# Where attention steps stand between the matmuls of a feed-forward layer: only after whole products, in groups, from the third run on

## The chip, the core and the metric

The kernel runs on one core of a Trainium2 chip. The core has five engines with a queue of instructions each: TensorE (PE in the profile, with PEld for the loading of its weights) does matmuls and transposes and writes PSUM; ScalarE (ACT) and VectorE (DVE) read PSUM and write on-chip memory or PSUM; GpSimd (POOL) here does pooling sums and normalisation; SyncE (SP) issues the DMAs. An engine works through its queue in order, and waits on semaphores for the others. The metric is the device time of the program in microseconds (us), less is better.

## The reference

Eight batches of attention with eight heads, whose keys and values are averaged over 8 neighbours (576 to 72), feed a two-layer network with a leaky ReLU over 4608 tokens:

```python
B, H, S, D = 8, 8, 576, 64
k_p = k.reshape(B, H, S // 8, 8, D).mean(axis=3)
v_p = v.reshape(B, H, S // 8, 8, D).mean(axis=3)
scores = np.matmul(q, k_p.transpose(0, 1, 3, 2)) / np.sqrt(D)
attn = softmax(scores)                  # max subtracted, 1e-9 added to the sum
x = heads_side_by_side(np.matmul(attn, v_p))          # 4608 x 512
h = x @ w_in                                          # 512 -> 2048
out = np.maximum(0.01 * h, h) @ w_out                 # 2048 -> 512
```

## The kernel before

**The feed-forward layer.** The tokens are cut into nine chunks of 512, the hidden width into 16 blocks `f` of 128. A block of a chunk is two products: `m1` (lines 621 to 641) makes the hidden block, twelve matmuls (four slices `kk` by three: each operand is split into a high and a low part and low times low is left out), then Prelu (L635) and a rounding copy `gh` (L638) on ACT and the rest `gl` on DVE (L639); `m2` (lines 643 to 660) adds the block's share to four accumulators, twelve matmuls as well, and comes two blocks later than the `m1` whose result it uses. Every product yields control twice: in its middle, after six matmuls (L633, L659), and at its end.

**Runs.** `runs` (L614) lists ten runs `n`: chunk 0 with blocks 0 to 7, chunk 1, chunk 0 with blocks 8 to 15, and then chunks 2 to 8, one run each. In the text "run 4, f13, m2" is the second product that is issued with block 13 of run 4.

**Attention steps.** While run `n` is at work, the attention that the next chunk needs is done in small steps, which `line_up` (L554) puts into a fixed order. The number behind the batch's name is the tile of up to 128 query rows, the last digit the half of the heads:

- `q` (L359): four transposes of a tile of q into PSUM, a copy `qT` on ACT (L365).
- `sa` (L367): four score matmuls into `pss`; DVE takes the maximum (L383), ACT takes exp, four times a pair of instructions (L385).
- `sb`: sums and reciprocals on DVE (L396, L397), normalisation `at` on POOL (L402, L406). It has no work on TensorE.
- `pu` (L417): three transposes of `at` into `pp`; from there ACT copies `pT_hi` (L429) and `rh` (L430), DVE makes `pT_lo` (L433) and `pT_rem` (L437).
- `au` (L443): for two pairs of heads each, four matmuls into `pa` that read `pT_hi`, `pT_lo`, `pT_hi` and `pT_rem` in this order (L453 to L456); ACT copies `xh` (L463), DVE makes `xl` (L464). It follows the last `pu` of its piece and half.
- `ku`, `vu` (L319, L333): keys and values of a new batch; `vu` is two pairs of matmuls into `pv` (L351), each followed by a DVE product (L354).
- `lk`, `lv`: the DMAs and POOL sums of a batch's keys and values; `fetch` and `tails` stand at the ends of run 2.

**What sets the order.** TensorE's order is the order of the source (`manual_schedule`, L749); the instructions of the other engines are put in order by the framework's scheduler. For a batch after the first every attention step takes its PSUM from one pool of two buffers (`ps_a`, L83, through `bank`, L208), in turn; `au`, `ku` and `vu` take both. `pT_hi`, `pT_lo` and `pT_rem` are single buffers. The loop at L766 counts beats, one for each yield, four for each block; at each beat it issues steps until their number reaches `len(us) * beat // (beats - 4)`. Runs 2 to 8 have 31 to 43 steps, run 2 in 32 beats, the others in 64. So before the change a beat gets one step or none, and a few beats of run 2 get two.

Of the kernel before, what the change touches and what calls it, by code (L numbers as in the profile page):

```python
# [24 lines left out]
def tile_pooled_attention_ffn(  # L25
# [595 lines left out]
    def m1(k):  # L621

        n, c, f = parts[k]
        xh, xl = x_parts(c)
        w = ws[0, f]
        nm = f"{c}_{f}"
        ph = ps_h.tile([P, CH], F32, tag="h", name=f"ph{nm}")
        for kk in range(NK):
            ks = slice(kk * P, (kk + 1) * P)
            nc.tensor.matmul(ph, w[:, 0, ks], xh[kk], start=kk == 0, stop=False)  # L630
            nc.tensor.matmul(ph, w[:, 0, ks], xl[kk], start=False, stop=False)  # L631
            nc.tensor.matmul(ph, w[:, 1, ks], xh[kk], start=False, stop=kk == NK - 1)  # L632
            if kk == 1:  # L633
                yield
        nc.scalar.activation(ph, ph, AF.Prelu, alpha=0.01)  # L635
        gh = three.tile([P, CH], F32R, tag="gh", name=f"gh{nm}")
        gl = three.tile([P, CH], F32R, tag="gl", name=f"gl{nm}")
        casts.append(nc.scalar.copy(gh, ph))  # L638
        nc.vector.tensor_tensor(gl, ph, gh.bitcast(F32), op=ALU.subtract)  # L639
        gs[k] = gh, gl  # L640
        yield

    def m2(k):

        n, c, f = parts[k]
        gh, gl = gs.pop(k)
        hi, lo = ws[1, f][:, 0, :], ws[1, f][:, 1, :]
        first, last = f == runs[n][1][0], f == runs[n][1][-1]
        for t in range(NT):
            if first:  # L650
                accs[t] = ps_acc.tile([P, DM], F32, tag=f"acc{t}", name=f"acc{n}_{t}")
            r = slice(t * P, (t + 1) * P)
            a = accs[t]
            nc.tensor.matmul(a, gh[:, r], hi, start=first, stop=False)  # L654
            nc.tensor.matmul(a, gh[:, r], lo, start=False, stop=False)  # L655
            nc.tensor.matmul(a, gl[:, r], hi, start=False, stop=last)  # L656
            if last:
                store(n, c, t, a)
            if t % 2:  # L659
                yield  # L660
# [40 lines left out]
    def convert_to(n):  # L701
        nonlocal stepped
        while stepped < min(int(n), len(steps)):
            steps[stepped]()
            stepped += 1
# [43 lines left out]
    with tc.manual_schedule(engines={nc.tensor.engine}):  # L749
        at, total = 0, len(parts)  # L750
        for n, (c, fs) in enumerate(runs):
            us = list(units[n])
            if n >= 2:
                mid = len(us) // 2
                for b in early[n]:
                    us[mid:mid] = [att[b]["lk"], att[b]["lv"]]
            beats, done, beat = 4 * len(fs), 0, 0
            for f in fs:
                if n == 0:
                    convert_to(14 + 2.8 * f)  # L760
                elif n == 1:
                    convert_to(36 + 3 * f)
                    if f == 11:
                        for b in early[1]:
                            att[b]["lk"]()
                            att[b]["lv"]()  # L766
                slots = [m1(at)] + ([m2(at - 2)] if at >= 2 else [])
                for slot in slots:
                    for _ in slot:
                        beat += 1  # L770
                        while done < min(len(us), len(us) * beat // (beats - 4)):
                            us[done]()
                            done += 1
                at += 1
            while done < len(us):
                us[done]()
                done += 1
        for at in (total - 2, total - 1):
            for _ in m2(at):
                pass  # L780
# [31 lines left out]
```

## Time and profile before

| | |
|---|---|
| runs shown | 1023.65, 1024.62, 1025.46 us; median 1024.62 |
| the profiled execution | 1024.45 us, of which 1022.7 us lie between the first and the last instruction (the span) |
| granted TensorE clock, mean | 0.971 |
| first weights and first attention, until run 2 | about 237 us |
| runs 2 to 9 | from there to the end |

The page of the profile gives busy time and share of the span for every engine, then slices, the chain of work that ended last, and groups of instructions. The timeline gives single instructions: start and duration in us, engine, line of the source, operation, output and inputs; "x3" stands for three instructions merged into one row, and a bracket says how long the engine had been idle and what released it. Matmuls overlap in it, since their ends are modelled: the pace of TensorE is read from start to start.

### The profile page before, as it was taken

What the parts mean: (1) busy time and instruction counts of PE and PEld (TensorE: products, weight loads), DVE (VectorE), ACT (ScalarE), POOL (GpSimd) and SP (SyncE); (2) the same over time, 40 slices, a digit from 0 to 9 for tenths busy, and PEclk for the clock granted to TensorE, in tenths of its full rate; (3) what the DMA queues carried; (4) which work ended last, traced back from release to release, by engine and by line L of the source; (5) the groups of instructions that cost most, each with busy time, mean ns of one, the idle gap of its engine ahead of it and who ended that gap; (6) DMA issues with size and microseconds to landing.
All of it is one profiled execution on the core that took longest, in us unless ns stands there. A gap on an engine that the chain in (4) does not pass through costs nothing.

```text
span 1022.7 us, 12812 instructions
## 1 busy us (share of the span) xinstructions
PE 963.4 (94%) x4568; PEld 785.4 (77%) x4568; DVE 363.6 (36%) x846; ACT 428.1 (42%) x1386; POOL 232.7 (23%) x336
## 2 busy tenths in 40 slices
PE   4566989989999999999999999999999999999998
PEld 4355778768887778878888788888887788888886
DVE  5787738413323332332232322232232322231111
ACT  4757755414534343534343434333443433342121
POOL 3576315520106620133012301022101001000000
PEclk8677999989999999999999999999999999999999
DMA  9556301322015410212012202020200020001001
GB/s 266 160 155 191 112 32 51 91 75 63 6 25 137 114 40 11 62 47 58 6 57 57 58 1 68 6 57 6 62 11 11 1 62 1 1 1 42 1 1 41
DMA packets 65007, 57.45 MB, mean 56 GB/s; under 512 B 39856, under 2 KB 48048, under 8 KB 64944
## 3 DMA queue, kind: packets, MB, share of 16 engines
q1 hardware_dynamic: 64944, 56.64, 19.2%
q8 instruction: 36, 0.59, 0.2%
q14 instruction: 27, 0.22, 0.1%
HBM read 46.14 MB, written 10.49 MB: 55 GB/s over the span
## 4 chain that ended last, share of the span: by engine, by line
PE 76%; DMA 2%; DVE 2%; ACT 1%; POOL 1%; issue 1%; SPq 0%; ACTq 0%; POOLq 0%; DVEq 0%
PE ph L630 12%; PE acc L654 11%; PE ph L632 11%; PE ph L631 11%; PE acc L656 11%; PE acc L655 11%; PE pss L375 3%; PE pp L427 2%; PE pq L363 1%; PE pa L453 1%; PE pa L456 1%; PE pa L454 1%; PE pa L455 1%; DVE w L196 0%; DMA kraw<-in_k_dram 0%
## 5 line engine op out<-in xcount | busy, mean ns | idle before, releaser
L630 PE MATMUL ph<-xh,w 128*128 128x512 f32 x576 | 236.9, 411 | 5.2 <-DVE gl L639 5.2
L654 PE MATMUL acc<-w,gh 128*128 128x512 f32 x576 | 234.6, 407 | 0.0
L631 PE MATMUL ph<-xl,w 128*128 128x512 f32 x576 | 227.3, 395 | 0.0
L632 PE MATMUL ph<-xh,w 128*128 128x512 f32 x576 | 227.2, 395 | 0.0
L656 PE MATMUL acc<-w,gl 128*128 128x512 f32 x576 | 225.7, 392 | 0.0
L655 PE MATMUL acc<-w,gh 128*128 128x512 f32 x576 | 225.6, 392 | 0.0
L635 ACT ACTIVATE ph<-ph 128x512 f32<-128x512 f32 x144 | 84.3, 585 | 287.4 <-PE ph L632 287.4
L639 DVE TENSOR_TENSOR gl<-ph,gh 128x512 fp32r<-128x512 f32 x144 | 99.4, 690 | 270.8 <-ACT gh L638 269.9
L402 POOL TENSOR_TENSOR at<-e,red 128x256 f32<-128x256 f32 (+1 forms) x76 | 47.4, 624 | 502.1 <-DVE red L397 370.0
L385 ACT ACTIVATE e<-pss,red 128x72 f32<-128x72 f32 (+1 forms) x320 | 98.2, 321 | 112.0 <-DVE red L383 110.9
L630 PEld LDWEIGHTS ph<-xh,w 128*128 128x128 f32 x576 | 109.6, 190 | 28.5 <-DVE gl L639 6.6
L632 PEld LDWEIGHTS ph<-xh,w 128*128 128x128 f32 x576 | 109.6, 190 | 24.3
L656 PEld LDWEIGHTS acc<-w,gl 128*128 128x128 f32 x576 | 108.4, 188 | 24.0
L654 PEld LDWEIGHTS acc<-w,gh 128*128 128x128 f32 x576 | 108.5, 188 | 21.7 <-issue 1.4
L631 PEld LDWEIGHTS ph<-xl,w 128*128 128x128 f32 x576 | 109.9, 191 | 19.5
L655 PEld LDWEIGHTS acc<-w,gh 128*128 128x128 f32 x576 | 108.7, 189 | 19.3
L638 ACT CAST gh<-ph 128x512 fp32r<-128x512 f32 x144 | 85.3, 592 | 3.0
L383 DVE TENSOR_REDUCE red<-pss 128x4 f32<-128x288 f32 (+1 forms) x80 | 36.2, 453 | 103.7 <-PE pss L375 102.7
L385 ACT ACTIVATION_READ_ACCUMULATOR e<-pss,red 128x1 f32 (+1 forms) x320 | 65.9, 206 | 0.0
L375 PEld LDWEIGHTS pss<-kT,qT 128*128 128x128 f32 (+1 forms) x320 | 49.5, 193 | 14.4 <-issue 3.5
L375 PE MATMUL pss<-kT,qT 128*128 128x144 f32 (+1 forms) x320 | 57.0, 307 | 3.0 <-ACT qT L365 1.8
L433 DVE TENSOR_TENSOR pT_lo<-pp,pT_hi 128x256 fp32r<-128x256 f32 (+1 forms) x80 | 31.6, 395 | 72.0 <-ACT rh L430 71.4
(85 smaller groups left out, 898.3 us busy)
## 6 DMA issues: line engine op xcount, KB each, us to landing
out_dram<-o SPq DMA_DIRECT2D x35, 256.0 KB, 2.2
kraw<-in_k_dram SPq DMA_DIRECT2D x32, 256.0 KB, 4.4
q<-in_q_dram SPq DMA_DIRECT2D x32, 256.0 KB, 3.0
vraw<-in_v_dram SPq DMA_DIRECT2D x32, 256.0 KB, 4.4
w_bits<-in_moe_w_in_dram SPq DMA_DIRECT2D x16, 512.0 KB, 4.0
w_bits<-in_moe_w_out_dram SPq DMA_DIRECT2D x16, 512.0 KB, 6.9
krem<-in_k_dram SPq DMA_DIRECT2D x8, 128.0 KB
vrem<-in_v_dram SPq DMA_DIRECT2D x8, 128.0 KB
```

The costliest lines, as they stand in the source:

```text
L375: nc.tensor.matmul(sc[:n, 2 * SP * i : 2 * SP * (i + 1)], qT[:, p, :n], kT[:, p, :, :].rearrange("d i s -> d (i s)"), start=True, stop=True,)
L385: ins = nc.scalar.activation(e[:n, h, :], scv[:n, h, :], AF.Exp, bias=mx[:n, h : h + 1], accum_out=sm[:n, h : h + 1],)
L402: eng.tensor_tensor(at[:n, 0:2, :].rearrange("a i (h s) -> a (i h) s", h=2), e[:n, :, 0:MAIN], sm[:n].unsqueeze(2).broadcast_to([n, 4, MAI ...
L630: nc.tensor.matmul(ph, w[:, 0, ks], xh[kk], start=kk == 0, stop=False)
L631: nc.tensor.matmul(ph, w[:, 0, ks], xl[kk], start=False, stop=False)
L632: nc.tensor.matmul(ph, w[:, 1, ks], xh[kk], start=False, stop=kk == NK - 1)
L635: nc.scalar.activation(ph, ph, AF.Prelu, alpha=0.01)
L638: casts.append(nc.scalar.copy(gh, ph))
L639: nc.vector.tensor_tensor(gl, ph, gh.bitcast(F32), op=ALU.subtract)
L654: nc.tensor.matmul(a, gh[:, r], hi, start=first, stop=False)
L655: nc.tensor.matmul(a, gh[:, r], lo, start=False, stop=False)
L656: nc.tensor.matmul(a, gl[:, r], hi, start=False, stop=last)
```

## The change

From run 2 on the loop goes on without issuing anything at odd beats, which are those in the middle of a product:

```diff
                     for _ in slot:
                         beat += 1
+                        if n >= 2 and beat % 2:
+                            continue
                         while done < min(len(us), len(us) * beat // (beats - 4)):
                             us[done]()
                             done += 1
```

The formula still counts all beats, so at an even beat the steps of the odd one before are issued too. The order of the steps stays as it is; each stands where it was or six matmuls later. In run 3, from block 11 on, with `|` for the middle and the end of each product:

```
            m1 mid | m1 end      | m2 mid | m2 end
before f11  sb11   |             | sa20   | pu10
       f12  sb20   |             | sa21   | pu20
       f13         | sb21        | au00   | pu01
       f14         | pu11        | pu21   | au01
after  f11         | sb11        |        | sa20 pu10
       f12         | sb20        |        | sa21 pu20
       f13         | sb21        |        | au00 pu01
       f14         | pu11        |        | pu21 au01
```

Of the 266 steps of runs 2 to 8, 130 stood in the middle of a product. Steps with matmuls or transposes of their own number 194. Before they stand at 192 places, two of which hold two of them; after at 163 places, of which 31 hold two of them. Between neighbouring places lie six matmuls of the feed-forward layer or more before, twelve or more after.

## The prediction

> **What bounds the kernel now.** I read the head of the page first (span), then TensorE's busy time over the stretch that the change touches (columns: stretch, its length, PE busy and instructions, granted clock, DMA share, GB/s), then the waits of PEld there (who waited for whom, us in total, times, longest).
>
> ```profile
> span 1022.7 us, 12812 instructions
> ...
> 240.00:1018.00 778.00, 774.72 (x3743) 1.00 0.13 35
> ...
> PEld pv L351 <- DVE xl L464: 2.8, 4, 1.2
> ...
> PEld pa L453 <- ACT e L385: 1.4, 3, 0.7
> ```
>
> From 240 us on TensorE is busy 774.72 of 778.00 us at a granted clock of 1.00. Its order is the order of the source, so a wait there moves everything behind it, and the end, by as much; no slack takes it up. The two largest waits for another engine are those of `vu` for `xl` (2.8 us) and of `au` for the exps of a score step (1.4 us). The other engines matter only through what TensorE waits for. The sum is made against the profiled execution: span 1022.7 us, 1024.45 us in all, which is 0.17 us under the median of the runs, 1024.62.
>
> **Does joining steps save anything?** The attention matmuls stay the same; the places at which TensorE changes over to them fall from 192 to 163. Rows of the timeline: start, duration, engine, line, operation.
>
> ```profile
> 111.67 0.60 PE L363 MATMUL pq<-ident,q 128*128 128x128 f32 x4
> 112.11 0.66 PE L375 MATMUL pss<-kT,qT 128*128 128x144 f32 x4
> 112.50 0.49 PE L630 MATMUL ph<-xh,w 128*128 128x512 f32 x1
> 112.84 0.40 PE L631 MATMUL ph<-xl,w 128*128 128x512 f32 x1
> ...
> 667.84 0.60 PE L363 MATMUL pq<-ident,q 128*128 128x128 f32 x4
> 668.19 0.48 PE L654 MATMUL acc<-w,gh 128*128 128x512 f32 x1
> 668.51 0.40 PE L655 MATMUL acc<-w,gh 128*128 128x512 f32 x1
> 668.74 0.40 PE L656 MATMUL acc<-w,gl 128*128 128x512 f32 x1
> ```
>
> Alone, `q` takes 668.19 - 667.84 = 0.35 us, and the product matmul behind it has 668.51 - 668.19 = 0.32 us to the next one, where 668.74 - 668.51 = 0.23 is the rule: 0.09 us for the return. Joined with an `sa` (run 0 has such groups), `q` takes 112.11 - 111.67 = 0.44 us: the 0.09 is paid between the two steps. So joining gains **0** as long as nothing waits. If each join did gain 0.09, 29 would be 2.6 us; I keep that for the range.
>
> **What the 31 groups hold.** By the order of `line_up`: ten join steps that don't depend on each other and need one buffer each (`sa` and `pu`, two `pu`, a `q` and an `sa` of another tile): 0. Twelve join a `pu` and the `au` that reads its result. Five have an `au` and then a step that wants the first buffer of that `au` back (one of them, run 2 f12, is a group already). Four are single: `q0 sa00` of the same tile (run 2 f8), `sa01 vu` (run 2 f9), `vu sa00` (run 3 f6) and `sa40 au10` (run 6 f5).
>
> **The twelve `pu au`.** Run 0 ends with such a group, of a tile with 64 rows; below it stand the same two steps of run 3 with six product matmuls between them:
>
> ```profile
> 139.58 0.40 PE L427 MATMUL pp<-ident,at 64*128 64x64 f32 x3
> ...
> 140.42 0.29 DVE L433 TENSOR_TENSOR pT_lo<-pp,pT_hi 128x128 fp32r<-128x128 f32 x1 [0.88 <-ACT rh L430]
> ...
> 140.77 0.41 PE L454 MATMUL pa<-pT_lo,v_hi 128*128 128x320 f32 x1
> ...
> 141.90 0.39 PE L630 MATMUL ph<-xh,w 128*128 128x512 f32 x1
> ...
> 394.04 0.40 PE L427 MATMUL pp<-ident,at 64*128 64x64 f32 x3
> 394.37 0.50 PE L654 MATMUL acc<-w,gh 128*128 128x512 f32 x1
> ...
> 395.86 0.31 PE L453 MATMUL pa<-pT_hi,v_hi 128*128 128x320 f32 x1
> ...
> 397.04 0.39 PE L630 MATMUL ph<-xh,w 128*128 128x512 f32 x1
> ```
>
> Joined, from the first transpose to the next product matmul go 141.90 - 139.58 = 2.32 us: `au` can't start its second matmul (L454, 140.77) before `pT_lo` is there (140.42 + 0.29 = 140.71). Apart, nothing waits: `pu` takes 394.37 - 394.04 = 0.33, `au` takes 397.04 - 395.86 = 1.18, and one return is 0.09. The join costs 2.32 - 0.33 - 1.18 - 0.09 = 0.72 us. Five of the twelve have a tile of 64 rows: 5 x 0.72 = **3.6 us**.
>
> For 128 rows the chain through ACT and DVE is longer. Its rows, at the end of `m2` (137.73) and at the end of `m1` (392.23), where Prelu stands ahead of it on ACT, and an `au` over 256 columns:
>
> ```profile
> 137.73 0.52 PE L427 MATMUL pp<-ident,at 128*128 128x128 f32 x3 [1.06 <-DVE x_tail L466]
> ...
> 138.86 0.42 DVE L433 TENSOR_TENSOR pT_lo<-pp,pT_hi 128x256 fp32r<-128x256 f32 x1 [0.69 <-ACT rh L430]
> ...
> 392.23 0.49 PE L427 MATMUL pp<-ident,at 128*128 128x128 f32 x3
> ...
> 392.47 0.49 PE L654 MATMUL acc<-w,gh 128*128 128x512 f32 x1
> ...
> 393.49 0.42 DVE L433 TENSOR_TENSOR pT_lo<-pp,pT_hi 128x256 fp32r<-128x256 f32 x1 [2.60 <-ACT rh L430]
> ...
> 605.57 0.28 PE L453 MATMUL pa<-pT_hi,v_hi 128*128 128x256 f32 x1
> ...
> 606.52 0.39 PE L630 MATMUL ph<-xh,w 128*128 128x512 f32 x1
> ```
>
> `pT_lo` is done 138.86 + 0.42 - 137.73 = 1.55 us after the first transpose, or 393.91 - 392.23 = 1.68. From there to the next product matmul it was 0.06 + (141.90 - 140.77) = 1.19 with 320 columns, where a matmul of `au` takes 1.18 / 8 = 0.148; with 256 it takes (606.52 - 605.57) / 8 = 0.119, so 1.19 less 6 x 0.029 = 1.02. Apart, it is 0.24 (392.47 - 392.23) + 0.95 + 0.09 = 1.28. Four groups at the end of `m2`: 4 x (1.55 + 1.02 - 1.28) = 4 x 1.29 = **5.2**. Three at the end of `m1`: 3 x (1.68 + 1.02 - 1.28) = 3 x 1.42 = **4.3**. Should the scheduler put the cast `gh` and `gl` ahead of the chain too, an `m1` group costs about 1.2 more; it didn't at 392 us.
>
> **The `au` with a step behind it.** The group that run 2 has already, at 270 us:
>
> ```profile
> 270.16 0.28 PE L453 MATMUL pa<-pT_hi,v_hi 128*128 128x256 f32 x1
> ...
> 271.71 0.55 PE L427 MATMUL pp<-ident,at 128*128 128x128 f32 x3
> 272.02 0.48 PE L654 MATMUL acc<-w,gh 128*128 128x512 f32 x1
> ```
>
> From the first matmul of `au` to the next product matmul go 272.02 - 270.16 = 1.86 us; apart it is 0.95 + 0.24, and one return less, so the wait for ACT's `xh` and DVE's `xl` of the first half is about 0.65. Four new groups: 4 x 0.65 = **2.6**. The old one moves to the end of `m2` and keeps its price.
>
> **The four single groups.** Rows: `q` and its copy; `vu` and its DVE product; an `au` 1.88 us behind an `sa`, whose second half waits for the buffer of that `sa`:
>
> ```profile
> 242.28 0.60 PE L363 MATMUL pq<-ident,q 128*128 128x128 f32 x4
> ...
> 242.91 0.59 ACT L365 COPY qT<-pq 128x512 f32<-128x512 f32 x1 [1.25 <-PE pq L363]
> ...
> 251.15 0.40 PE L351 MATMUL pv<-vremparts,spread 32*128 32x64 f32 x2
> ...
> 251.59 0.42 DVE L354 TENSOR_TENSOR v_rem<-pv,heads 128x256 fp32r<-128x256 f32 x1 [0.19 <-PE pv L351]
> ...
> 647.57 0.65 PE L375 MATMUL pss<-kT,qT 128*128 128x144 f32 x4
> ...
> 649.45 0.28 PE L453 MATMUL pa<-pT_hi,v_hi 128*128 128x256 f32 x1
> ...
> 650.53 0.39 PE L453 MATMUL pa<-pT_hi,v_hi 128*128 128x256 f32 x1 [0.45 <-ACT e L385]
> ```
>
> - `q0 sa00`: the copy ends 242.91 + 0.59 - 242.28 = 1.22 us after the first transpose; joined, `sa` would start at 0.44. With 0.06 for the semaphore and the 0.1 by which the first step behind a wait was longer (1.13 against 7 x 0.148 above): **0.9**.
> - `vu sa00`: the first buffer is free 251.59 + 0.42 - 251.15 = 0.86 after `vu` starts, and `sa` would start at about 0.4: **0.6** with the same 0.16.
> - `sa40 au10`: the second half of `au` starts 650.53 - 647.57 = 2.96 after `sa`. It would start 0.47 (half of 0.95) after the first half, which came at 649.45; so it waits 0.6 now. Joined, the first half comes 1.4 earlier (six matmuls) and the buffer not: up to 1.4 more, and at least 1.1, since at the end of `m2` the maximum doesn't stand behind `gl`. I take **1.3**.
> - `sa01 vu`: the same wait for the same buffer: **1.3**.
>
> **What goes.** `vu` in runs 3, 4 and 7 stands six matmuls behind the `au` whose buffers it wants, and after the change twelve. In the waits quoted first, 2.8 us are of this kind. `au10` in run 7 gets twelve behind its `sa` as well, 0.4 of the 1.4 us. Together **-3.2**. If the new place of the DVE and ACT work kept these waits, they would cost 0 to 3.2 more than I count.
>
> **What moves along at no cost.** `sb` has no work on TensorE; its DVE and POOL work moves six matmuls at most, and `at` is read by a `pu` at least two products later. `lk` and `lv` (POOL sums, and DMAs on SP's queue) and each `q`'s load two tiles ahead move by at most 1.4 us, ahead of uses that are ten and more us away. The last step of a run stays at its beat, two products before the next run reads `xh` and `xl`. What lies in neighbouring groups stands twelve matmuls, 2.7 us, apart, more than the 1.68 us in which a `pu` at the end of `m1` has its `pT_lo`.
>
> **Sum.** 3.6 + 5.2 + 4.3 + 2.6 + 0.9 + 0.6 + 1.3 + 1.3 - 3.2 = **+16.6 us**; 1024.6 + 16.6 = **1041.2 us**.
>
> **The rivals.**
>
> *Faster: waits go and none come.* Joining would gain its 2.6 us, and 3.2 us of waits go: 1024.6 - 5.8 = 1018.8. It needs the chains to hide: from the point where `pT_lo` is done within the 0.36 us that `pu` and the first matmul of `au` take, not in 1.55. The rows above speak against it, since the group at 139.58 did wait. 5%. The Trainium skill (Perfetto Trace Analysis, Matmul Optimizations) advises to issue matmuls back-to-back in batches, which would favour the change; the joined `q` above shows no gain from it.
>
> *The waits are longer.* If ACT and DVE take the groups at the end of `m1` behind `gh` and `gl` (six groups that wait there, 1.2 each) and the longer queues reach the next group at every third join (10 x 0.4), it is 11 more: 1052. For it: two steps' work arrives at once. Against: ACT and DVE were idle before these rows (0.88 us before `pT_lo` at 140.42). 17%.
>
> *The waits are about half.* If a `pu` that is joined gets its ACT and DVE work at once, ahead of everything, and the waits of `vu` go entirely: near 1032. 10%.
>
> *The clock falls.* Behind a long pause the pace is halved:
>
> ```profile
> 78.00:90.00 12.00, 3.85 (x14) 0.73 0.71 228
> ...
> 90.30 0.63 PE L632 MATMUL ph<-xh,w 128*128 128x512 f32 x1
> 90.72 0.63 PE L654 MATMUL acc<-w,gh 128*128 128x512 f32 x1
> ```
>
> After 12 us with 3.85 of them busy, product matmuls are 90.72 - 90.30 = 0.42 us apart instead of 0.23, for about twelve of them: 2.4 us. If each of the 18 new waits did so, that is 43 us more: 1084. Against it: the stretch from 240 us has waits of `vu` of up to 1.2 us and a granted clock of 1.00 throughout. 3%. The Trainium skill (TensorE: Matmul & The Clock Gate, A second HAM failure mode) tells of a kernel in which cycling through PSUM buffers made the clock swing by such short pauses; by that rule it would be this case, and the rows so far don't agree.
>
> *Nothing happens.* If the waits that come and go cancelled, or the steps did not move: 1024.6. The beats are counted four to a block in every run from 2 on, so odd ones are the middles, and the order of TensorE is the source's: 3%.
>
> **Chances and range.** The forecast, 1035 to 1048: 62%; longer waits 17%, half 10%, clock 3%, nothing 3%, faster 5%. The range takes in the bounds of the unknown prices (the `m1` groups, the waits that go) and most of both neighbours: 1031 to 1054. A measurement of this kernel can tell about 0.2% (2 us) from no change: faster 5%, within 0.2% 3%, slower 92%.
>
> **What would show it.** In the trace after: waits of `pa` L453 and L454 for `pT_hi` and `pT_lo` twelve times, some 1 us each before the loading; of `pp` for `xl` five times; one `pss` behind `qT`; no long wait of `vu` in runs 3, 4 and 7; TensorE idle some 14 us more in the stretch from 240 us, and its clock at 1.00. I am wrong if `au` behind `pu` starts without a wait, if the clock falls, or if waits show up between groups, where I count none.

## The result and the profile after

| | before | after |
|---|---|---|
| median of four runs each, us | 1024.69 | 1037.85 |
| lowest to highest, us | 1023.65 to 1025.46 | 1036.72 to 1038.16 |
| the profiled execution, us | 1024.45 | 1038.16 |
| its span, us | 1022.7 | 1036.4 |

The kernel became slower: the ratio of after to before is 1.0118, with a 95% interval of 1.0105 to 1.0131, which is 10.8 to 13.4 us; by the medians it is 13.2 us (the ratio is an estimate of its own and not the quotient of the two medians, which is 1.0128). The forecast was 16.6 us more, 1041.2.

The head of the page of after, and then TensorE over the stretch that the change touches (length, PE busy and instructions, granted clock, DMA share, GB/s):

```profile
span 1036.4 us, 12814 instructions
```

```profile
240.00:1032.00 792.00, 779.40 (x3745) 1.00 0.13 35
```

The instructions are the same but for two (12812 before), and the clock is 1.00 over the whole stretch, as before. TensorE is idle 792.00 - 779.40 = 12.60 us in it, against 3.28. The waits of its matmuls there (who waited for whom, us in total, times, longest):

```profile
PE pa L453 <- ACT pT_hi L429: 5.7, 12, 0.6
PE pp L427 <- DVE xl L464: 1.8, 4, 0.5
PE pa L454 <- DVE pT_lo L433: 1.7, 7, 0.2
PE pa L453 <- DVE xl L464: 0.9, 1, 0.9
PE pss L375 <- ACT qT L365: 0.7, 1, 0.7
PE pv L351 <- DVE v_rem L354: 0.5, 1, 0.5
PE pq L363 <- DVE xl L464: 0.4, 1, 0.4
PE pv L351 <- DVE xl L464: 0.2, 1, 0.2
```

The first and third row are the twelve groups `pu au`: each waits for `pT_hi`, and the seven with a tile of 128 rows wait a second time, for `pT_lo`. The second and seventh are groups of `au` and a step behind it: five, four `pp` and one `pq`. The fourth is `sa40 au10`, `pss` behind `qT` is `q0 sa00`, and the two of `pv` are `sa01 vu` and a `vu` in run 3. The waits of `vu` for `xl` have shrunk: the loading of its weights waited 2.8 us, and now this much:

```profile
PEld pv L351 <- DVE xl L464: 0.7, 2, 0.4
```

The matmuls' waits add up to 11.9 us, and yet the time grew by 13.2 with the waits of before gone. So such a list gives the places, not the price. The price is read from start to start. First a group at the end of `m1` with the work of ACT and DVE, then the ends of one of 64 rows, one at the end of `m2`, one of `au` and `pu`, and `q0 sa00` (start, duration, engine, line, operation, and in brackets how long the engine was idle before and for what):

```profile
286.44 0.49 PE L427 MATMUL pp<-ident,at 128*128 128x128 f32 x3
286.64 0.58 ACT L635 ACTIVATE ph<-ph 128x512 f32<-128x512 f32 x1 [0.83 <-PE ph L632]
...
287.13 0.38 ACT L429 CAST pT_hi<-pp 128x256 fp32r<-128x256 f32 x1
...
287.55 0.62 ACT L638 CAST gh<-ph 128x512 fp32r<-128x512 f32 x1
...
287.56 0.38 PE L453 MATMUL pa<-pT_hi,v_hi 128*128 128x256 f32 x1 [0.63 <-ACT pT_hi L429]
287.71 0.42 DVE L433 TENSOR_TENSOR pT_lo<-pp,pT_hi 128x256 fp32r<-128x256 f32 x1 [1.48 <-ACT rh L430]
...
288.19 0.38 PE L454 MATMUL pa<-pT_lo,v_hi 128*128 128x256 f32 x1 [0.24 <-DVE pT_lo L433]
...
289.14 0.39 PE L654 MATMUL acc<-w,gh 128*128 128x512 f32 x1
...
612.23 0.40 PE L427 MATMUL pp<-ident,at 64*128 64x64 f32 x3
...
614.36 0.39 PE L630 MATMUL ph<-xh,w 128*128 128x512 f32 x1
...
719.05 0.49 PE L427 MATMUL pp<-ident,at 128*128 128x128 f32 x3
...
721.59 0.40 PE L630 MATMUL ph<-xh,w 128*128 128x512 f32 x1
...
273.02 0.28 PE L453 MATMUL pa<-pT_hi,v_hi 128*128 128x256 f32 x1
...
274.58 0.55 PE L427 MATMUL pp<-ident,at 128*128 128x128 f32 x3 [0.45 <-DVE xl L464]
274.89 0.48 PE L630 MATMUL ph<-xh,w 128*128 128x512 f32 x1
...
244.11 0.60 PE L363 MATMUL pq<-ident,q 128*128 128x128 f32 x4
245.38 0.76 PE L375 MATMUL pss<-kT,qT 128*128 128x144 f32 x4 [0.68 <-ACT qT L365]
245.88 0.49 PE L630 MATMUL ph<-xh,w 128*128 128x512 f32 x1
```

The first group takes 289.14 - 286.44 = 2.70 us where its two steps take 1.28 apart: 1.42 lost, of which the brackets show 0.63 + 0.24 = 0.87. The rest stands in records that count as busy: the modelled end of the transposes reaches into the wait, and a matmul behind a wait is recorded with 0.38 us instead of 0.28. ACT works in the order Prelu (286.64), `pT_hi` (287.13), `rh`, `gh` (287.55), so `gh` did not get ahead of the chain. At the end of `m2` the group takes 721.59 - 719.05 = 2.54; the tile of 64 rows 614.36 - 612.23 = 2.13; the `au` with a `pu` behind it 274.89 - 273.02 = 1.87.

Taken so over every place from run 2 on (from the start of the last product matmul ahead of it to that of the second one behind it, less twice their own pace of 0.227 us), the places of attention cost about 116.4 us before and 129.9 after, +13.5. From the first `ku` of run 2 to the last matmul it is +13.2, between the two spans +13.7.

### The profile page after: what moved, and what is told of

Read it like the earlier page. It is cut to its first block, busy times and chain, and to the rows that moved or that the text cites. A ratio compares the mean times of both kernels' runs of the same rounds, so it can differ in the third digit from the quotient of the medians.

```text
span 1036.4 us, 12814 instructions
## 1 busy us (share of the span) xinstructions
PE 967.1 (93%) x4568; PEld 785.7 (76%) x4568; DVE 362.2 (35%) x846; ACT 426.4 (41%) x1386; POOL 233.2 (23%) x336
## 4 chain that ended last, share of the span: by engine, by line
PE 76%; DVE 2%; DMA 2%; ACT 2%; POOL 1%; issue 1%; SPq 0%; POOLq 0%; ACTq 0%
PE ph L630 11%; PE acc L654 11%; PE ph L632 11%; PE ph L631 11%; PE acc L656 11%; PE acc L655 11%; PE pss L375 3%; PE pp L427 2%; PE pq L363 1%; PE pa L454 1%; PE pa L456 1%; PE pa L455 1%; PE pa L453 1%; DVE w L196 0%; DMA vraw<-in_v_dram 0%
```

## The experiments

The line numbers in the rows of a changed kernel are its own; the operation's name tells which step it is. In each, time is compared with that of the kernel before on the same chip.

**Are the twelve groups the loss?** One kernel takes them out of after, and one puts only them into before. `follows` is true for the `au` that reads what the last `pu` of its piece makes. `e1_pu_apart`, in the loop of after:

```diff
-                        if n >= 2 and beat % 2:
-                            continue
-                        while done < min(len(us), len(us) * beat // (beats - 4)):
+                        upto = min(len(us), len(us) * (beat + beat % 2) // (beats - 4))
+                        if n >= 2 and beat % 2:
+                            cut = [i + 1 for i in range(done, upto - 1)
+                                   if follows(us[i][0], us[i + 1][0])]
+                            upto = cut[0] if cut else done
+                        elif n < 2:
+                            upto = min(len(us), len(us) * beat // (beats - 4))
+                        while done < upto:
```

> The changed kernel, but in the twelve groups of a `pu` and the `au` that reads its result the `pu` goes six matmuls earlier, where it stood before. Theory (the wait of these twelve groups is nearly the whole loss; read from single groups of the trace they cost 13.0 us): 1037.9 - 13.0 = 1024.9 us. Rival (the loss goes with grouping as such, spread over the 31 groups): 12/31 of 13.2, so about 1032.8 us.

`e2_pu_joined_only`, in the loop of before:

```diff
-                        while done < min(len(us), len(us) * beat // (beats - 4)):
+                        upto = min(len(us), len(us) * beat // (beats - 4))
+                        if n >= 2 and beat % 2:
+                            then = min(len(us), len(us) * (beat + 1) // (beats - 4))
+                            if done < upto < then and follows(us[upto - 1][0], us[upto][0]):
+                                upto -= 1
+                        while done < upto:
```

> The kernel before, with nothing changed but that the `pu` of these twelve groups waits for the end of the product and stands right ahead of its `au`. Theory: 1024.7 + 13.0 = 1037.7 us, as much as the whole change. Rival (spread over the groups): 1024.7 + 5.1 = 1029.8 us.

Measured: without the groups 1025.35 us against 1025.54, ratio 0.9995 (0.9982 to 1.0007); with the groups alone 1036.26 against 1025.54, ratio 1.0118 (1.0103 to 1.0133). By the ratio that is the whole loss of the change. By the medians it is 10.7 us, less than the 13.0 expected; by the profiled executions, from the first `ku` of run 2 to the last matmul, it is 12.9 us, and by starts each of the twelve costs in `e2_pu_joined_only` what it costs in after, within 0.02 us. In the waits of TensorE in `e2_pu_joined_only` the groups have after's numbers:

```profile
PE pa L453 <- ACT pT_hi L429: 5.7, 12, 0.6
```

What follows: twelve of the 31 groups carry the loss. The other parts of the change, with signs of both kinds, cancel within the interval.

**What do they wait for: the data, or the buffers?** The prediction says data: `au` reads what ACT and DVE make of `pp`. But `au` also takes both buffers, and one of them is `pp`. `e3_no_data` lets the `au` of the twelve groups read weights of the feed-forward layer in place of `pT`:

```diff
+        if (b, j, g) in JOINED:
+            pc = {"hi": ws[1, 0], "lo": ws[1, 1], "rem": ws[1, 2][:, 0, :]}
```

> The changed kernel, but in the twelve groups `au` reads weights that have long been in place instead of `pT_hi`, `pT_lo` and `pT_rem` (the output then lacks the attention of these halves). Theory A (the wait is for the data, as the prediction has it): the twelve cost nothing, 1024.9 us. Theory B (two PSUM buffers are too few for three uses in a row: the second half of `au` waits until `pT_rem` is made from the buffer of `pu`, or until `xl` is made from its own first half, and both come about 1.8 us after `pu` starts, as late as the data did): 1037 us, between 1034 and 1039.

Measured: 1036.45 against 1025.54, ratio 1.0114 (1.0099 to 1.0129). Without the data little was gained: by starts the twelve groups cost 12.0 us in place of 13.0. The waits of TensorE in its trace, and then the second half of an `au` in its timeline (L456 is the first matmul of a half, `pT_rem` the last reader of `pp`):

```profile
PE pa L456 <- DVE pT_rem L438: 9.3, 12, 1.1
```

```profile
284.87 0.49 PE L428 MATMUL pp<-ident,at 128*128 128x128 f32 x3
285.12 0.37 PE L456 MATMUL pa<-w,v_hi 128*128 128x256 f32 x1
...
286.97 0.36 PE L456 MATMUL pa<-w,v_hi 128*128 128x256 f32 x1 [1.14 <-DVE pT_rem L438]
```

The first half starts right behind the transposes, and the second half waits until `pp` has been read, for nearly as long. So there are two waits with one end: either alone holds the group. To show it, the buffer had to go as well. `e4_no_data_one_buffer` puts both halves of these `au` (256 columns each) into one buffer:

```diff
-            pa = bank(b, f"pa{b}_{j}_{p}")
-            pa = pa.rearrange("a p x -> a (p x)")[:, :w]
+            if (b, j, g) in JOINED and w == 256:
+                if i == 0:
+                    both = bank(b, f"pa{b}_{j}_{g}").rearrange("a p x -> a (p x)")
+                pa = both[:, w * i : w * (i + 1)]
+            else:
+                pa = bank(b, f"pa{b}_{j}_{p}")
+                pa = pa.rearrange("a p x -> a (p x)")[:, :w]
```

> As the run without the data, and besides both halves of `au` (2 x 256 columns) go into one PSUM buffer in the ten groups where they fit, so that `pu` and `au` need two buffers in all (output as in that run). Theory A: 1024.9 us, as without this. Theory B: the ten go to nothing and the two with 320 columns keep about 0.75 each: 1026.4 us. If neither data nor buffer is what they wait for: 1037 us.

Measured: 1043.51 against 1025.54, ratio 1.0183 (1.0164 to 1.0203), slower than all that was expected. The experiment had put in a wait of its own: in one buffer the second half waited until ACT and DVE had read the first, up to 2.0 us, as TensorE's waits show (eleven of them: the ten groups, and `sa40 au10`, which waits 0.9 us in after too):

```profile
PE pa L461 <- DVE xl L472: 13.3, 11, 2.0
```

So it says nothing on the question. The next two kernels issue, in the ten groups, all eight matmuls of the `au` first, and what reads them behind: `e5_no_data_one_buffer_2` with the weights in place of `pT`, `e6_one_buffer` with `pT` itself.

```diff
-        for i in range(2):
-            p = 2 * g + i
...
+        if one:
+            products(0)
+            products(1)
+            reads(0)
+            reads(1)
+        else:
+            for i in range(2):
+                products(i)
+                reads(i)
```

> As the earlier run without the data and with one buffer for both halves of `au`, but all eight matmuls of `au` now come ahead of the copies that read them (before, the second half's matmuls had to wait for the reading of the first half, since they share the buffer). Output as there. If data and buffer are all that the twelve groups wait for, ten of them go to nothing: the kernel before + 13.2 - 11.4 = + 1.8 us. If something else holds them, + 11 us, as without the data alone.

> The changed kernel with the one buffer for both halves of the `au` of the ten groups, matmuls first, and with its data. The data chain alone must then make the wait, and it ends as late as the buffer did: the kernel before + 13 us, between + 12 and + 14. If the buffer were what counts alone: + 1.8 us.

Measured: with neither wait 1026.37 against 1025.05, ratio 1.0009 (1.0000 to 1.0019), or 0 to 1.9 us; with the data alone 1038.29, ratio 1.0123 (1.0104 to 1.0142). Of the waits of the groups, this is left in the first, for two `au` with 320 columns that still took two buffers:

```profile
PE pa L464 <- DVE pT_rem L438: 0.8, 2, 0.5
```

The second has the twelve waits for `pT_hi` of after, 5.7 us, although its matmuls stand in the same order as in the first: it is not the order that took the waits away.

What follows: data and buffers together are what the twelve groups wait for, and each is enough. Another buffer for `au` alone would not have helped.

**Which buffer does a step get?** For two single groups the prediction counted 1.3 us each, on the ground that the two buffers are taken in turn. `e8_two_scores_joined` is before with these two alone (`follows` is true for `sa40 au10` and `sa01 vu`, the loop is that of `e2_pu_joined_only`):

```diff
+    def follows(u, w):
+        return (u, w) in (("5.sa40", "5.au10"), ("2.sa01", "2.vu"))
```

> The kernel before, with nothing changed but that `sa40` of batch 5 and `sa01` of batch 2 wait for the end of the product and stand right ahead of `au10` and `vu`. If buffers are taken in turn, as the prediction had it, the second half of `au` and of `vu` must wait for the exps of that `sa`: 1.3 more each, the kernel before + 2.6 us, and the trace shows the second L453 and L351 released by ACT's exps. If the buffer that comes free first is taken, the second half waits for `xl` or `v_rem` of its own first half: + 0.5 us, and the trace shows DVE as the releaser.

Measured: 1027.17 against 1026.03, ratio 1.0010 (0.9998 to 1.0022), at most 2.3 us, so not 2.6. The rows of its timeline with the second halves:

```profile
651.01 0.37 PE L453 MATMUL pa<-pT_hi,v_hi 128*128 128x256 f32 x1
...
652.66 0.38 PE L453 MATMUL pa<-pT_hi,v_hi 128*128 128x256 f32 x1 [0.92 <-DVE xl L464]
...
653.15 0.22 ACT L385 ACTIVATION_READ_ACCUMULATOR e<-pss,red 128x1 f32 x1
...
252.17 0.40 PE L351 MATMUL pv<-vremparts,spread 32*128 32x64 f32 x2 [0.55 <-DVE v_rem L354]
```

The second half of `au` waits for `xl` of its own first half, and the second pair of `vu` for `v_rem` of its first: neither waits for the exps of the `sa` ahead. In the first group the last exp is read out at 653.15, when the second half has already started (652.66). By starts, the group `sa40 au10` costs 0.47 us more than its steps apart, `sa01 vu` 0.02. From the first `ku` of run 2 to the last matmul its profiled execution is 2.6 us longer than that of before, which looks like the first theory; but up to 1.7 us of that is a fall of the clock at 343 us (last section), which lies at neither of the two groups.

**Can the waits go altogether?** `e7_spaced` is before, with a rule that holds a step back until the steps it would wait for are far enough behind, counted in beats of six matmuls:

```diff
+    APART = {
+        "q": {"au": 1, "vu": 1},
+        "sa": {"au": 1, "vu": 1, "q": 1},
+        "pu": {"au": 1, "vu": 1, "pu": 1},
+        "ku": {"au": 1, "vu": 1, "sa": 1},
+        "au": {"pu": 1, "sa": 2, "au": 1, "vu": 1},
+        "vu": {"au": 2, "sa": 2},
+    }
...
                         while done < min(len(us), len(us) * beat // (beats - 4)):
-                            us[done]()
+                            step = us[done][0].split(".")[-1].rstrip("0123456789")
+                            if n >= 2 and any(beat - seen.get(x, -9) < far
+                                              for x, far in APART.get(step, {}).items()):
+                                break
+                            us[done][1]()
+                            seen[step] = beat
```

> The kernel before with every beat open, but a step is held until it stands clear of those it waits for: `au` one beat behind its `pu` and two behind an `sa`, `vu` two behind an `au` or an `sa`, and nothing in the same beat behind an `au` or a `vu`. By the waits of the trace of before that this takes away (three of `vu` on `xl` 2.9, `vu` behind `sa01` 0.9, `au10` behind an `sa` 0.7 and 0.4, `pu01` behind `au00` 0.7): 5.6 us under the kernel before. If these waits only move to the next step: no difference.

Measured: 1019.05 us (1017.74 to 1019.46) against 1025.05, ratio 0.9936 (0.9922 to 0.9949): the fastest of all. All waits of its matmuls from 240 us on:

```profile
PE acc L654 <- DVE o L677: 0.3, 1, 0.3
PE pv L351 <- DVE xl L464: 0.3, 1, 0.3
```

From the first `ku` of run 2 (238.25) to the last matmul (1011.45) it takes 773.20 us, against 1017.52 - 240.05 = 777.47 before: 4.3 us of the gain lie there. The other 1.8 us of the two traces lie ahead of 240 us, where nothing was changed; the first `ku` came between 238.97 and 240.72 us in the other nine traces of this study, with the same work ahead of it. Whether all of the 6.0 us by the medians come from the rule is thus not settled; 4.3 us are shown, where 5.6 were expected.

## Why the prediction came out

It was right in direction, in range and in the pairs that it named, and 3.4 us too high (16.6 for 13.2 by the medians; the table's 13.5 is that of the two profiled executions). Of the mechanism it had one half. Its steps, with the cost of each join by starts in the trace of after:

| step of the prediction | predicted, us | measured, us |
|---|---|---|
| five `pu au` of 64 rows | 3.6 | 3.8 |
| four `pu au` at the end of `m2` | 5.2 | 5.0 |
| three `pu au` at the end of `m1` | 4.3 | 4.2 |
| four new `au` with a step behind | 2.6 | 2.5 |
| `q0 sa00` | 0.9 | 0.9 |
| `vu sa00` | 0.6 | 0.6 |
| `sa40 au10` | 1.3 | 0.5 |
| `sa01 vu` | 1.3 | 0.0 |
| waits that go | -3.2 | -3.4 |
| ten independent joins, and what is left | 0 | -0.6 |
| sum | 16.6 | 13.5 |

- **The twelve groups** came out within 0.2 us in each kind, from rows of run 0 and of single steps of before. That `gh` stays behind the chain held as well. The reason was half of it: the prediction named the data, but the buffers hold the groups as long (`e3_no_data`, `e5_no_data_one_buffer_2`).
- **The step that failed** is that of `sa40 au10` and `sa01 vu`, 2.6 us for 0.5. It put their second halves behind the exps of the `sa` ahead, because the two buffers were said to be taken in turn; the description of the kernel says so too, and is wrong there. In these traces a step gets the buffer that comes free first. In before, the second half of `au10` did wait for the exps (650.53), since `xh` stood behind them on ACT and the buffer of the first half, read by `xl` behind `xh`, came free later still. Joined, the first half is done before the exps begin, `xh` goes ahead of them on ACT, and the wait becomes one for `xl`. For `vu`, the wait for `v_rem` was there before the change and stays. The rows of after:

```profile
253.49 0.40 PE L351 MATMUL pv<-vremparts,spread 32*128 32x64 f32 x2 [0.55 <-DVE v_rem L354]
...
347.19 0.41 PE L351 MATMUL pv<-vremparts,spread 32*128 32x64 f32 x2
347.80 0.41 PE L351 MATMUL pv<-vremparts,spread 32*128 32x64 f32 x2 [0.20 <-DVE xl L464]
348.13 0.76 PE L375 MATMUL pss<-kT,qT 128*128 128x144 f32 x4
...
657.14 0.37 PE L453 MATMUL pa<-pT_hi,v_hi 128*128 128x256 f32 x1
...
657.91 0.37 ACT L463 CAST xh<-pa 128x256 fp32r<-128x256 f32 x1 [2.48 <-PE pa L456]
658.18 0.33 ACT L385 ACTIVATE e<-pss,red 128x72 f32<-128x72 f32 x1
...
658.79 0.38 PE L453 MATMUL pa<-pT_hi,v_hi 128*128 128x256 f32 x1 [0.92 <-DVE xl L464]
```

- **`vu sa00`** has the predicted size by luck, since it comes by another way. `pss` (348.13) doesn't wait, so the buffer of `vu` was not its trouble; instead `vu` still waits for the `xl` of an `au` twelve matmuls ahead (347.80), where the prediction counted that wait as gone. The 0.6 is the group's cost less that of the two steps apart, and holds this wait. `e7_spaced` has 0.3 of it in the row quoted above.
- **The waits that go** were sized well, -3.4 for -3.2, and **joining** gains little: most joins of independent steps are paid as the row of run 0 said. That row is one of 128 rows, and the return behind a step of 64 rows costs more, about 0.2 us: two of the ten joins have two such steps, pay it once, and gain 0.2 each (a `q` and an `sa` cost 0.59 and 0.84 at 776.99 and 778.98 in before and 1.23 together at 789.20 in after). They make 0.4 of the 0.6; the other eight gain 0.07 at most.
- **"TensorE idle some 14 us more"** was the wrong thing to look for: it is 12.60 - 3.28 = 9.3 us. The rest of the loss is in records that count as busy, as in the group at 286.44 us.
- **The rivals.** Half the waits (1032) would have needed the chain of `pu` to go ahead of Prelu; Prelu was first (286.64). Longer waits (1052) would have needed `gh` ahead of the chain, and waits between neighbouring groups; the list has one of these, the 0.2 us of `vu` at 347.80, which the prediction had not counted. The clock stayed at 1.00 in after. The swings of the clock behind frequent short pauses, of which the Trainium skill tells (TensorE: Matmul & The Clock Gate, A second HAM failure mode), didn't come here, though the clock can fall behind a short pause, see the last section. The Trainium skill also advises to issue matmuls back-to-back in batches (Perfetto Trace Analysis, Matmul Optimizations); here they were back-to-back before, 774.72 of 778.00 us, and the joined steps had to wait: 1.2% more.

## What to carry to other kernels

When steps are to be moved next to each other on an engine that is never idle, look at pairs: a step that reads, through other engines, what the one before it wrote costs most of the length of that chain, and independent neighbours cost nothing and gain little. Price the pair from start to start, from a place where the trace already has it; idle time alone understates it. Before a second buffer is added or the data come earlier, ask whether another wait ends at the same time, and to find waits worth removing, space dependent steps apart by rule, as `e7_spaced` does.

## What the runs showed of the hardware

**The clock can fall after a single wait of about 1 us, or not.** The list of after has pauses of up to 0.9 us and its clock never moved. Before has this one in front of `vu`, with the clock at 1.00 behind it:

```profile
341.75 0.41 PE L351 MATMUL pv<-vremparts,spread 32*128 32x64 f32 x2 [1.12 <-DVE xl L464]
```

The same pause stands in `e8_two_scores_joined`, and there the clock fell: first rows of the timeline, then windows of 2 us (length, PE busy, granted clock, DMA share, GB/s):

```profile
341.89 0.41 PE L351 MATMUL pv<-vremparts,spread 32*128 32x64 f32 x2 [1.14 <-DVE xl L464]
...
343.02 0.63 PE L654 MATMUL acc<-w,gh 128*128 128x512 f32 x1
343.45 0.63 PE L655 MATMUL acc<-w,gh 128*128 128x512 f32 x1
```

```profile
340.00:342.00 2.00, 0.86 (x5) 1.00 0.06 15
342.00:344.00 2.00, 2.00 (x8) 0.75 0.45 87
344.00:346.00 2.00, 2.00 (x8) 0.50 0.80 229
346.00:348.00 2.00, 2.00 (x9) 0.89 0.59 156
```

Product matmuls are 343.45 - 343.02 = 0.43 us apart in place of 0.23. The windows give 2.00 x (0.25 + 0.50 + 0.11) / 0.5 = 3.4 us at half the clock, so about 1.7 us lost at most. `e4_no_data_one_buffer` has two such falls, at 280.27 and 290.51 us, behind waits of 1.98 and 1.84 us. The Trainium skill (TensorE: Matmul & The Clock Gate, What's actually happening) describes a free-running window of about 3.4 us, and takes one idle window for the fall; the length at half pace agrees with that. The pause in front of it was a good deal shorter here.

The packed traces also record when the granted clock changed. In all ten of them each change stands a whole multiple of 3.413 us behind the one before it: in `e8_two_scores_joined` the fall at 343.01 us comes 35 of them behind the rise at 223.54. So in these traces the clock changes at the ends of fixed intervals only. Where the pause stood in its interval does not explain why it brought the clock down in one execution and not in the other, since it began about 1.2 us behind the start of an interval in both. What the three falls have in common is an interval with little work: by the columns of the matmuls that start in it, they are the three emptiest of all traces between 240 and 1010 us (2432, 2560 and 2816 columns). The interval in before comes next, with the same matmuls as that of `e8_two_scores_joined` and one more on its very edge, while a wait of 1.84 us in `e4_no_data_one_buffer` (700.69), in an interval with 3968 columns, brought no fall. Where the limit lies was not tested.
